# First tile of products in quarters, second pair of chunks one after the other, inverse matmuls spread over more steps

## The chip, the cores and the metric

The kernel runs on one core of a Trainium2 chip. A core has a matrix engine (TensorE, "PE"; its weight loads are listed apart as "PEld"), a vector engine (VectorE, "DVE"), an engine for activation functions (ScalarE, "ACT"), a general one (GpSimd, "POOL") and a sequencer that mostly issues transfers (SyncE, "SP"). Each works through its own instructions in order and waits at semaphores for the others. 16 DMA engines move data between DRAM and the on-chip memories SBUF and PSUM; transfers issued by SP and ACT go to hardware queues, those issued by POOL to a software queue. The metric is the device time of one execution in microseconds (us), lower is better.

## The reference

```python
xn = layernorm(x)                                  # x: 2048 x 1024, over the last axis
X  = rfft2(xn) * (w_r + 1j * w_i)                  # w_r, w_i: 2048 x 513
s  = irfft2(X, (2048, 1024))
g  = silu(silu(xn @ w1) @ w2)                      # w1: 1024 x 3584, w2: 3584 x 1024
out = x + s * g
```

All inputs and the output are float32.

## The kernel before

**Numbers.** Each float32 operand of a matmul is split into a high and a low float16 part, and three products are added: high x high, high x low, low x high. The high part is an ACT copy with a scale (`high`, line 228), the low part a DVE subtraction (`low`, line 231). Weights are scaled by powers of two per tile: `maxi` takes each row's largest magnitude on DVE, `scales` adds these maxima over the rows with a small PE matmul (line 235) and computes the scale in a few small DVE instructions (lines 256 to 265).

**Tiles.** The 2048 rows of x form four chunks c of 512 rows, each of four parts p of 128. A chunk is normalized and transposed into `xnT[c]` (high and low). Chunks 0 and 1 are transposed on PE (`trans`, then `hi` on ACT and `lo` on DVE, through two PSUM buffers "tp"); chunks 2 and 3 by DMA transposes that SP issues (`turned`, line 633). The 3584 columns of w1 form 28 tiles f of 128. A tile of the first product, `mm1(c, f)`, is 24 matmuls of 128x512 (8 slices of the inner dimension, three terms); ACT applies silu to its PSUM result (line 441) and `hidden` makes from two neighbouring f and two neighbouring chunks the sums and differences of a Strassen-like scheme, splits them ("hosum" and "hoone", one buffer each) and stores them to DRAM ("hd"). The second product, `mm2`, goes through seven such products m of eight tiles j, each in two halves of 21 matmuls; `acc` adds its results up, and `final` finishes output rows.

**Spectral part.** Forward transform along the rows (`fa_mat`, `fd_gen`), along the columns with the filter (`f_gen`), then the inverse, `i_gen(c)`, for the chunks in the order 1, 3, 0, 2. `i_gen` loads "zt" and a table, copies a few edge values into zt on ACT (line 1133), does four matmul groups `mat(0..3)` (line 1146, 48 matmuls each, PSUM tiles "iu" from the pool `pt` with two buffers), each followed by `post` (its PSUM tile is last read at line 1157), `split`, and then four groups `mat2` and `bfly` (last instruction line 1225). The edge values of all chunks come from a small job, `edge_gen`, mostly on POOL.

**Order.** The program is written out in order by one loop over `order`, the list of (c, f). After each tile (and after each half tile of `mm2`) one event takes place: ACT and DVE work left over from the last tiles is issued, then stores that are due (`tick`), then `work()` takes one step of the queue `wq` (weights), in three of four events one of `xq` (maxima, edges), and up to three of `bg` (layer norm of later chunks, forward, filter, inverse). A generator that yields PAUSE ends the event; other yields name no wait. Steps of `bg` are also held back by a count of PE and DVE time that the program keeps from its own instructions (`meter`, line 190). An instruction stands in its engine's stream where its event stands.

**The start.** Lines 1338 to 1361: x parts 0 and 1, the identity matrix, x parts 2 and 3, then raw w1 tiles 0 to 3 are loaded by SP; `spin` issues matmuls without use, 35 at first and 8, 8, 8 and 12 between the steps of layer norm and weights. Tile (0,0) is one `mm1` with all terms; in event 0 the sums of w1 tiles 2 and 3 (`scales(2, 2)`) are issued, and then tile (0,1).

**Order of tiles.** (0,0..3), (1,0..3), (0,4), (0,5), (1,4), (1,5), then for f = 0, 2, 4: (2,f), (2,f+1), (3,f), (3,f+1); then for every further pair of f all four chunks. `finish(bg, ln[c])` before a chunk's first tile forces its layer norm to be issued by then. Raw w1 tiles from 6 on are loaded only when chunk 3 has used earlier ones (`ahead`, `used1`), and w1 raw and split tiles share seven buffers.

**Stores.** `stores[0]` is the engine that issues the stores of hidden, forward and filter results; here it is POOL throughout.

Of the kernel before, what the change touches and what calls it, by code (L numbers as in the profile page):

```python
# [10 lines left out]
F32 = mybir.dt.float32  # L11
# [10 lines left out]
WARM = [35, 8, 0, 8, 0, 8, 12, 0, 0, 0]  # L22
# [82 lines left out]
def spectral_ffn(ctx, tc, x, w_r, w_i, w1, w2, ca, kc, ci, tw, pm, out):  # L105
# [40 lines left out]
    deferred, stores = [], [nc.gpsimd]  # L146
# [91 lines left out]
    def weights1():  # L238
# [30 lines left out]
        def split(i):  # L269
            new[i] = fp.tile([128, 2, 8, 128], F16, name=f"w1_{i}", tag="w1", bufs=7)  # L270
            high(new[i][:, 0], raw[i], rs[:, i:i + 1])
# [5 lines left out]
        for i in range(4):  # L277
            load(i)
        yield 0
        maxi(0)  # L280
        yield 0
        maxi(1)
        yield 0
        scales(0, 2)
        yield 0
        split(0)
        rest(0)
        yield 0
        split(1)
        rest(1)  # L290
# [133 lines left out]

    def mm1(c, f):
        ps = pf.tile([128, 512], F32, name=f"pa{c}_{f}", tag="ff")
        w, xt = w1t[f], xnT[c]
        terms = [(d, wh, xh) for wh, xh in ((0, 0), (0, 1), (1, 0)) for d in range(8)]
        if c + f:
            terms.sort(key=lambda k: k[0])  # L430
        for n, (d, wh, xh) in enumerate(terms):
            nc.tensor.matmul(ps, w[:, wh, d], xt[:, xh, d], start=(n == 0), stop=(n == 23))  # L432
        if c == 3:
            used1.add(f)
        q, g = f // 2, c // 2

        def evac():
            if (q, g) not in h32:
                h32[q, g] = H["p"].tile([128, 4, 512], F32, name=f"h32_{q}_{g}", tag="h32", bufs=2)
            hq = h32[q, g]  # L440
            nc.scalar.activation(hq[:, 2 * (c % 2) + f % 2], ps, AF.Silu, scale=s1[:, f:f + 1])  # L441
            if c % 2 and f % 2:
                return hidden(q, g)

        return evac
# [209 lines left out]
    def ln_gen(c):  # L655
# [33 lines left out]
        if c == 0:  # L689
            for p in range(2):  # L690
                stats(p)
                norm[p]()
            trans(0)
            hi(0)
            stats(2)
            norm[2]()
            trans(1)
            hi(1)
            stats(3)
            norm[3]()  # L700
            lo(0)
            yield 0
            trans(2)
            hi(2)
            lo(1)
            yield 0
            trans(3)
            hi(3)
            yield 0
            lo(2)  # L710
            lo(3)
            yield 0
            return
# [410 lines left out]
    def i_gen(c):  # L1124
        ip = C["p"]
        tt, stt = nc.vector.tensor_tensor, nc.vector.scalar_tensor_tensor
        if c != IORDER[0]:
            for _ in range(3):
                yield PAUSE
        else:  # L1130
            finish(xq, edge_job[0])
        zt, k = C["z"].pop(c), C["k"].pop(c)
        nc.scalar.activation(zt[:, :, :, :, 12, 0], zp[:, c], AF.Copy)
        yield PAUSE
# [104 lines left out]
        for i in range(6):  # L1239
            if i < 4:  # L1240
                mat(i)
            if i >= 2:
                split(i - 2)
            if 1 <= i <= 4:
                post(i - 1)
            yield 3.9 if 2 <= i <= 4 else 2
# [50 lines left out]
    with tc.manual_schedule():  # L1297
# [51 lines left out]
        for i in range(2):  # L1349
            load_x(0, i)  # L1350
        nc.sync.dma_start(ident, pm[:, 3])
        for i in range(2, 4):
            load_x(0, i)
        w1j = add(wq, weights1())
# [4 lines left out]
        for k, q in enumerate((bg, wq, bg, wq, bg, wq, wq, bg, wq)):  # L1359
            slot(q)  # L1360
            spin(WARM[1 + k])
# [10 lines left out]
        order += [(c, f + i) for f in (0, 2, 4) for c in (2, 3) for i in range(2)]  # L1372
# [4 lines left out]
        for n, (c, f) in enumerate(order):  # L1377
            left -= 1
            if f == 0 and c:
                finish(bg, ln[c])  # L1380
            if ln[3].done and n >= 22 and not f_job:
# [4 lines left out]
                add(bg, switch(B, open_i, 3, lag=2))  # L1386
# [118 lines left out]
```

## Time and profile before

| | us |
|---|---|
| median of 3 runs (lowest to highest) | 1272.59 (1272.42 to 1274.44) |
| profiled execution | 1271.76 |
| its span, first to last instruction | 1270.0 |

In the profile, busy time is given per engine. A line of a timeline has start, duration, engine, line of the program, operation, output and inputs, and in brackets the idle time of the engine before it with the instruction that ended it. Names are those of the program's tiles: "pa" is the PSUM tile of a first product, "tp" of a transpose, "iu" of an inverse group, "w1r" raw weights of w1, "jr" raw weights of w2 (both loaded from the tensor called B_w in the names), "h" a first product after silu. The table of windows gives for each stretch its length, then the busy time and count of PE, PEld, DVE, ACT and POOL, then PEclk (the TensorE clock that was granted, 1.00 is full), the DMA engines' mean busy share, and GB/s.

### The profile page before, as it was taken

How to read it: one execution, taken by the hardware profiler on the slowest of the kernel's cores; microseconds unless marked ns; L12 is line 12 of the kernel's file. 1: busy time of each engine (PE TensorE's matmuls, PEld its weight loads, DVE VectorE, ACT ScalarE, POOL GpSimd, SP SyncE). 2: the span in 40 equal slices, each digit the busy share in tenths (PEclk: the TensorE clock that was granted, in tenths of full speed). 3: DMA queues.
4: the chain of work that ended last, by engine and by line, in shares of the span. 5: the costliest groups of instructions: out<-in, count | busy, mean ns of one | idle time of the engine just before them, and what ended most of it. 6: DMA issues, size and time to landing. Idle time of an engine off the chain costs nothing. (4 is left out here: it accounts for less than half of the span.)

```text
span 1270.0 us, 20677 instructions
## 1 busy us (share of the span) xinstructions
PE 1229.6 (97%) x7759; PEld 625.0 (49%) x7759; DVE 1019.9 (80%) x2056; ACT 499.4 (39%) x672; POOL 330.1 (26%) x540
## 2 busy tenths in 40 slices
PE   8997999999999999999999999997998998999998
PEld 5543455455454444445545555544544545545544
DVE  6677889999998997565958799894776858978965
ACT  4755343434364465444534444241212212232211
POOL 1352132133454444342332021214023041010000
PEclk9998999999999999999999999999999999999999
DMA  7478366576477798776988799959388699893798
GB/s 234 129 160 212 96 199 185 159 224 190 116 272 239 227 300 297 241 226 187 223 249 261 217 274 247 263 200 331 141 252 252 225 309 318 309 358 124 265 348 292
DMA packets 155460, 296.87 MB, mean 234 GB/s; under 512 B 32048, under 2 KB 77744, under 8 KB 154848
## 3 DMA queue, kind: packets, MB, share of 16 engines
q1 hardware_dynamic: 118000, 179.82, 45.7%
q0 software_dynamic: 37216, 115.60, 28.9%
q8 instruction: 61, 1.00, 0.3%
q14 instruction: 39, 0.32, 0.1%
q10 hardware_dynamic: 144, 0.13, 0.0%
HBM read 186.97 MB, written 104.33 MB: 229 GB/s over the span
## 5 line engine op out<-in xcount | busy, mean ns | idle before, releaser
L432 PE MATMUL pa<-xnT,w 128*128 128x512 f16 x2688 | 586.5, 380 | 10.5 <-DMA xnT<-xs 6.2
L432 PEld LDWEIGHTS <-w 128*128 128x128 f16 x2688 | 262.6, 98 | 322.8 <-issue 12.5
L510 PE MATMUL pb<-w,ht 128*128 128x512 f16 (+1 forms) x798 | 299.9, 376 | 0.0
L511 PE MATMUL pb<-w,ht 128*128 128x512 f16 (+1 forms) x798 | 299.6, 375 | 0.0
L512 PE MATMUL pb<-w,ht 128*128 128x512 f16 (+1 forms) x798 | 299.5, 375 | 0.0
L512 PEld LDWEIGHTS <-ht 128*128 128x128 f16 x798 | 78.1, 98 | 91.3 <-issue 0.3
L510 PEld LDWEIGHTS <-ht 128*128 128x128 f16 x798 | 78.1, 98 | 89.6 <-issue 0.4
L511 PEld LDWEIGHTS <-ht 128*128 128x128 f16 x798 | 78.1, 98 | 87.5
L441 ACT ACTIVATE h<-pa,s 128x512 f32<-128x512 f32 x112 | 75.2, 677 | 89.3 <-PE pa L432 89.3
L231 DVE SCALAR_TENSOR_TENSOR w<-jr,sc,w 128x512 f16<-128x512 f32 x98 | 72.1, 749 | 38.7 <-ACT w L228 38.5
L228 ACT ACTIVATE w<-jr,sc 128x512 f16<-128x512 f32 x98 | 68.5, 714 | 78.9 <-DMA jr<-in_B_w_dram 72.1
L388 POOL DMA_DIRECT2D jr<-in_B_w_dram x56 | 37.5, 671 | 233.4 <-issue 175.6
L464 POOL DMA_DIRECT2D hd_sum<-hosum x56 | 41.5, 783 | 190.2 <-DVE hosum L231 75.3
L952 ACT ACTIVATE zq<-Z 128x192 f16<-128x192 f32 (+2 forms) x80 | 37.2, 543 | 104.3 <-DVE Z L218 67.2
L231 DVE SCALAR_TENSOR_TENSOR hoone<-h,hs,hoone 128x2048 f16<-128x2048 f32 x28 | 65.7, 2347 | 14.8 <-ACT hoone L228 14.8
L228 ACT ACTIVATE hosum<-hr,hs 128x1536 f16<-128x1536 f32 x28 | 44.0, 1573 | 80.3 <-DVE hr L471 62.8
L228 ACT ACTIVATE hoone<-h,hs 128x2048 f16<-128x2048 f32 x28 | 56.0, 1999 | 47.4 <-DMA hd_one<-hoone 24.9
L464 POOL DMA_DIRECT2D hd_one<-hoone x56 | 48.5, 866 | 71.8 <-DVE hoone L231 36.0
L470 DVE TENSOR_TENSOR hr<-h 128x1024 f32<-128x1024 f32 x28 | 34.2, 1223 | 39.9 <-ACT h L441 39.8
L231 DVE SCALAR_TENSOR_TENSOR hosum<-hr,hs,hosum 128x1536 f16<-128x1536 f32 x28 | 50.8, 1815 | 3.8 <-ACT hosum L228 3.8
L228 ACT ACTIVATE w<-w1r,rs 128x1024 f16<-128x1024 f32 x28 | 31.9, 1144 | 52.4 <-DVE rs L259 29.7
L591 ACT ACTIVATE pl<-pl,c 128x512 f32<-128x512 f32 (+1 forms) x26 | 17.0, 684 | 79.3 <-DVE pl L570 52.7
(215 smaller groups left out, 1815.9 us busy)
## 6 DMA issues: line engine op xcount, KB each, us to landing
jr<-in_B_w_dram POOLq DMA_DIRECT2D x84, 256.0 KB, 7.3
w1r<-in_B_w_dram SPq DMA_DIRECT2D x28, 512.0 KB, 5.9
hd_sum<-hosum POOLq DMA_DIRECT2D x56, 256.0 KB, 4.0
hd_one<-hoone POOLq DMA_DIRECT2D x56, 256.0 KB, 5.3
hd_dif<-hoone POOLq DMA_DIRECT2D x56, 256.0 KB, 5.0
w2m<-in_B_w_dram SPq DMA_DIRECT2D x28, 512.0 KB, 5.5
ht<-hd_dif SPq DMA_DIRECT2D x32, 448.0 KB, 10.3
ht<-hd_sum SPq DMA_DIRECT2D x32, 448.0 KB, 5.7
```

Source lines behind the costliest of these rows:

```text
L228: nc.scalar.activation(hi, raw, AF.Copy, scale=scale)
L231: nc.vector.scalar_tensor_tensor(lo, raw, scale, hi, op0=OP.mult, op1=OP.subtract)
L388: nc.gpsimd.dma_start(raw[n], ws[m][q] if m in ws else w2_block(m, q, 0))
L432: nc.tensor.matmul(ps, w[:, wh, d], xt[:, xh, d], start=(n == 0), stop=(n == 23))
L441: nc.scalar.activation(hq[:, 2 * (c % 2) + f % 2], ps, AF.Silu, scale=s1[:, f:f + 1])
L464: defer(1, lambda k=k, m=m: stores[0].dma_start(hd[m, g][:, :, q].rearrange("f p h s -> f p (h s)"), o[:, k].rearrange("f p h s -> f p (h ...
L470: tt(sums[:, 0:2], hq[:, 0::2], hq[:, 1::2], op=OP.subtract)
L510: nc.tensor.matmul(ps, hh[:, 0], w[:, 0], start=first, stop=False)
L511: nc.tensor.matmul(ps, hh[:, 0], w[:, 1], start=False, stop=False)
L512: nc.tensor.matmul(ps, hh[:, 1], w[:, 0], start=False, stop=last)
L591: nc.scalar.activation(o, o, AF.Silu, scale=c2)
L952: nc.scalar.activation(o[0], z, AF.Copy)
```

## The change

- The identity matrix is loaded between x parts 0 and 1, and raw w1 tile 0 ahead of x parts 2 and 3. Scales and split of w1 tiles 0 and 1 are made one tile at a time.
- Tile (0,0) is made by `quarter(p, k)`: 128 of its 512 columns (part p of the chunk) for one of the three terms k, eight matmuls of 128x128 each, into one PSUM tile. The twelve quarters are placed between the steps of layer norm and weights, and `mm1(0, 0)` issues no matmul. Idle matmuls are 35 and 8 now.
- Tiles of chunks 2 and 3 with f from 0 to 5: all four of chunk 2, then four of chunk 3, then two and two.
- `stores[0]` is SP until the layer norm of chunk 3 has been issued, then POOL.
- In `i_gen`, for all chunks but the first in order, the copy into zt is issued two pauses earlier, with three pauses behind it; steps 1 and 2 of the matmul groups end in a pause; and two more pauses come ahead of the first chunk.

```diff
--- before.py
+++ after.py
@@ -19,7 +19,7 @@
 S, D, F, DF = 2048, 1024, 3584, 513
 NFT = F // 128
 NP = NFT // 2
-WARM = [35, 8, 0, 8, 0, 8, 12, 0, 0, 0]
+WARM = [35, 8]
 LEAD, PAUSE, LAST, EARLY = 1.0, -1, 6, 2
 IORDER = (1, 3, 0, 2)
 SUMMED = (4, 5)
@@ -143,7 +143,7 @@
     turn2 = cp.tile([128, 128], F32, name="turn2")
     s_sc = small("s_sc")
 
-    deferred, stores = [], [nc.gpsimd]
+    deferred, stores = [], [nc.sync]
 
     def defer(n, fn):
         deferred.append([n, fn])
@@ -268,26 +268,26 @@
 
         def split(i):
             new[i] = fp.tile([128, 2, 8, 128], F16, name=f"w1_{i}", tag="w1", bufs=7)
+            first.setdefault("w", new[i])
             high(new[i][:, 0], raw[i], rs[:, i:i + 1])
 
         def rest(i):
             w1t[i] = w = new.pop(i)
             low(w[:, 1], raw.pop(i), rs[:, i:i + 1], w[:, 0])
 
-        for i in range(4):
+        load(0)
+        yield 0
+        for i in range(1, 4):
             load(i)
         yield 0
-        maxi(0)
-        yield 0
-        maxi(1)
-        yield 0
-        scales(0, 2)
-        yield 0
-        split(0)
-        rest(0)
-        yield 0
-        split(1)
-        rest(1)
+        for i in range(2):
+            maxi(i)
+            yield 0
+            scales(i, 1)
+            split(i)
+            yield 0
+            rest(i)
+            yield 0
         maxi(2)
         maxi(3)
         yield 0
@@ -422,14 +422,25 @@
 
     done2, ready2, chunks = [0], [-1], [0]
 
+    first = {}
+
+    def quarter(p, k):
+
+        if "ps" not in first:
+            first["ps"] = pf.tile([128, 512], F32, name="pa0_0", tag="ff")
+        sl = slice(128 * p, 128 * p + 128)
+        wh, xh = ((0, 0), (0, 1), (1, 0))[k]
+        for d in range(8):
+            nc.tensor.matmul(first["ps"][:, sl], first["w"][:, wh, d], xnT[0][:, xh, d, sl], start=(p + k + d == 0), stop=(p + k == 5 and d == 7))
+
     def mm1(c, f):
-        ps = pf.tile([128, 512], F32, name=f"pa{c}_{f}", tag="ff")
-        w, xt = w1t[f], xnT[c]
-        terms = [(d, wh, xh) for wh, xh in ((0, 0), (0, 1), (1, 0)) for d in range(8)]
+        ps = first["ps"] if c + f == 0 else pf.tile([128, 512], F32, name=f"pa{c}_{f}", tag="ff")
         if c + f:
+            w, xt = w1t[f], xnT[c]
+            terms = [(d, wh, xh) for wh, xh in ((0, 0), (0, 1), (1, 0)) for d in range(8)]
             terms.sort(key=lambda k: k[0])
-        for n, (d, wh, xh) in enumerate(terms):
-            nc.tensor.matmul(ps, w[:, wh, d], xt[:, xh, d], start=(n == 0), stop=(n == 23))
+            for n, (d, wh, xh) in enumerate(terms):
+                nc.tensor.matmul(ps, w[:, wh, d], xt[:, xh, d], start=(n == 0), stop=(n == 23))
         if c == 3:
             used1.add(f)
         q, g = f // 2, c // 2
@@ -690,24 +701,25 @@
             for p in range(2):
                 stats(p)
                 norm[p]()
-            trans(0)
-            hi(0)
+            for p in range(2):
+                trans(p)
+                hi(p)
+            yield 0
             stats(2)
+            yield 0
             norm[2]()
-            trans(1)
-            hi(1)
             stats(3)
-            norm[3]()
             lo(0)
-            yield 0
             trans(2)
             hi(2)
+            yield 0
+            norm[3]()
             lo(1)
-            yield 0
             trans(3)
             hi(3)
             yield 0
             lo(2)
+            yield 0
             lo(3)
             yield 0
             return
@@ -1124,14 +1136,14 @@
     def i_gen(c):
         ip = C["p"]
         tt, stt = nc.vector.tensor_tensor, nc.vector.scalar_tensor_tensor
-        if c != IORDER[0]:
-            for _ in range(3):
-                yield PAUSE
+        if c == IORDER[0]:
+            finish(xq, edge_job[0])
         else:
-            finish(xq, edge_job[0])
+            yield PAUSE
         zt, k = C["z"].pop(c), C["k"].pop(c)
         nc.scalar.activation(zt[:, :, :, :, 12, 0], zp[:, c], AF.Copy)
-        yield PAUSE
+        for _ in range(1 if c == IORDER[0] else 3):
+            yield PAUSE
         psu, uf, us = {}, {}, {}
 
         def mat(g):
@@ -1243,7 +1255,7 @@
                 split(i - 2)
             if 1 <= i <= 4:
                 post(i - 1)
-            yield 3.9 if 2 <= i <= 4 else 2
+            yield PAUSE if i in (1, 2) else 3.9 if i in (3, 4) else 2
         if c != IORDER[-1]:
             load_i(IORDER[IORDER.index(c) + 1])
         yield PAUSE
@@ -1346,19 +1358,44 @@
         nc.scalar.activation(warm, ones[:, 0:1], AF.Silu)
         J = {}
         open_fwd()
-        for i in range(2):
-            load_x(0, i)
+        load_x(0, 0)
         nc.sync.dma_start(ident, pm[:, 3])
+        load_x(0, 1)
+        w1j = add(wq, weights1())
+        slot(wq)
         for i in range(2, 4):
             load_x(0, i)
-        w1j = add(wq, weights1())
         slot(wq)
         ln = [add(bg, ln_gen(0)), None, None, None]
         nc.gpsimd.memset(mhalf, -0.5)
         spin(WARM[0])
-        for k, q in enumerate((bg, wq, bg, wq, bg, wq, wq, bg, wq)):
-            slot(q)
-            spin(WARM[1 + k])
+        slot(bg)
+        slot(wq)
+        slot(bg)
+        spin(WARM[1])
+        slot(wq)
+        quarter(0, 0)
+        quarter(1, 0)
+        slot(bg)
+        slot(wq)
+        quarter(0, 1)
+        slot(bg)
+        quarter(2, 0)
+        quarter(1, 1)
+        slot(wq)
+        quarter(0, 2)
+        quarter(1, 2)
+        slot(bg)
+        slot(wq)
+        quarter(3, 0)
+        quarter(2, 1)
+        quarter(2, 2)
+        slot(bg)
+        slot(wq)
+        quarter(3, 1)
+        quarter(3, 2)
+        slot(wq)
+        slot(bg)
         for i in range(4):
             load_x(1, i)
             if i == 1:
@@ -1369,7 +1406,7 @@
             add(bg, fd_gen(c))
 
         order = [(c, f) for fs in ((0, 1, 2, 3), (4, 5)) for c in range(2) for f in fs]
-        order += [(c, f + i) for f in (0, 2, 4) for c in (2, 3) for i in range(2)]
+        order += [(c, f) for fs in ((0, 1, 2, 3), (4, 5)) for c in (2, 3) for f in fs]
         order += [(c, f + i) for f in range(6, NFT - LAST, 2) for c in range(4) for i in range(2)]
         order += [(2 * g + c, f + i) for g in range(2) for f in range(NFT - LAST, NFT, 2) for c in range(2) for i in range(2)]
         last_use = {c: max(n for n, k in enumerate(order) if k[0] == c) for c in range(4)}
@@ -1378,12 +1415,14 @@
             left -= 1
             if f == 0 and c:
                 finish(bg, ln[c])
+            if ln[3].done:
+                stores[0] = nc.gpsimd
             if ln[3].done and n >= 22 and not f_job:
                 add(xq, wmax_gen())
                 max_job = add(xq, w2max_gen())
                 f_job = add(bg, switch(A, open_f, 1, max_job))
                 add(bg, f_gen())
-                add(bg, switch(B, open_i, 3, lag=2))
+                add(bg, switch(B, open_i, 5, lag=2))
                 for k in IORDER:
                     add(bg, i_gen(k))
             if left == 2 * LAST + 3:
```

## The prediction

> **What bounds the kernel now.** First the page: the span and the engines' shares.
>
> ```profile
> span 1270.0 us, 20677 instructions
> ...
> PE 1229.6 (97%) x7759; PEld 625.0 (49%) x7759; DVE 1019.9 (80%) x2056; ACT 499.4 (39%) x672; POOL 330.1 (26%) x540
> ```
>
> TensorE (PE) is busy for 97%, so the number of products bounds the kernel, and the change takes none away: 24 products of 512 columns become 96 of 128. What it can win is the 40.4 us in which PE stands (1270.0 - 1229.6) and what follows from standing. The table of PE's waits names them (us in total, times, longest):
>
> ```profile
> PE iu L1146 <- ACT zt L1133: 11.2, 3, 5.8
> PE iu L1146 <- DVE uw L1157: 6.5, 5, 3.4
> PE pa L432 <- DMA xnT<-xs: 6.2, 2, 5.7
> PE pa L432 <- ACT h L441: 1.9, 1, 1.9
> ...
> PE fa L742 <- DVE xnT L686: 1.5, 1, 1.5
> ```
>
> The first two stand ahead of and between the inverse matmuls (17.7 us), the next two around tile (3,0) of the first products (8.1 us). What follows from standing is in the windows' PEclk column, the third number from the end (the last two are the DMA share and GB/s):
>
> ```profile
> 108.00:112.00 4.00, 0.41 (x1) 0.21 (x2) 3.90 (x9) 3.48 (x3) 0.00 (x0) 0.54 1.12 236
> 114.00:117.00 3.00, 3.00 (x13) 1.23 (x12) 3.00 (x16) 0.00 (x0) 1.70 (x3) 0.81 0.21 62
> 877.00:881.00 4.00, 4.00 (x96) 3.87 (x92) 2.23 (x5) 1.32 (x2) 2.11 (x4) 0.66 1.02 394
> 962.00:970.00 8.00, 6.55 (x155) 5.10 (x156) 5.60 (x14) 1.89 (x5) 2.90 (x4) 1.00 1.07 325
> 1046.00:1050.00 4.00, 3.94 (x90) 3.94 (x92) 2.68 (x4) 0.73 (x2) 1.43 (x2) 0.62 1.09 312
> ```
>
> The stops that go with them, in PE's timeline (start, duration, in brackets the idle time before and its releaser):
>
> ```profile
> 876.83 4.22 PE L1146 MATMUL iu<-kk,zt 64*128 64x128 f16 x96 [5.79 <-ACT zt L1133]
> ...
> 962.68 2.85 PE L1146 MATMUL iu<-kk,zt 64*128 64x128 f16 x96 [2.81 <-ACT zt L1133]
> ...
> 1046.07 4.48 PE L1146 MATMUL iu<-kk,zt 64*128 64x128 f16 x96 [2.60 <-ACT zt L1133]
> ...
> 1053.95 2.74 PE L1146 MATMUL iu<-kk,zt 64*128 64x128 f16 x48 [3.41 <-DVE uw L1157]
> ```
>
> After the stops at 876 and 1046, and around (3,0), the granted clock is 0.54 to 0.81 for some microseconds; after the one at 962 it is 1.00, and the same 96 products take 2.85 there against 4.22 and 4.48. A removed stop can give back up to 1.6 beyond its own length. The 1.5 of fa stays: the statistics ahead of it keep their place behind the dense start.
>
> **The start.** Timeline, start and duration in us:
>
> ```profile
> 9.03 0.70 DVE L661 BATCH_NORM_STATS2 st<-x 128x6 f32<-128x512 f32 x1 [1.83 <-DMA x<-in_A_x_dram]
> ...
> 11.87 1.17 DVE L686 TENSOR_TENSOR xnT<-tp,xnT 128x1024 f16<-128x1024 f32 x1
> ...
> 13.02 1.00 ACT L682 ACTIVATE xnT<-tp 128x1024 f16<-128x1024 f32 x1
> ...
> 13.19 1.14 PE L678 MATMUL tp<-ident,x 128*128 128x128 f32 x8 [1.34 <-ACT x L669]
> 13.93 1.23 ACT L669 ACTIVATE x<-x,v 128x1024 f32<-128x1024 f32 x1
> ...
> 17.60 0.16 DVE L256 TENSOR_SCALAR e<-s 128x2 int32<-128x2 int32 x1 [1.18 <-PE s L235]
> ...
> 18.41 2.19 ACT L228 ACTIVATE w<-w1r,rs 128x1024 f16<-128x1024 f32 x2 [0.77 <-DVE rs L259]
> ...
> 19.59 1.28 DVE L231 SCALAR_TENSOR_TENSOR w<-w1r,rs,w 128x1024 f16<-128x1024 f32 x1 [0.83 <-ACT w L228]
> ...
> 24.25 2.34 DVE L251 TENSOR_REDUCE m<-w1r 128x1 f32<-128x1024 f32 x2
> ...
> 26.73 0.35 PE L235 MATMUL s<-m,ones 128*128 128x2 f32 x2
> ...
> 26.95 10.52 PE L432 MATMUL pa<-xnT,w 128*128 128x512 f16 x48
> ```
>
> Dense work begins at 26.95, when the column sums of w1 tiles 2 and 3 have passed PE. These sums wait for the two maxima on VectorE (DVE), at 24.25 to 26.59. After the change the sums still stand ahead of tile (0,1) on PE, and the maxima still come last on DVE, so an early first tile moves nothing unless DVE ends sooner. Its idle time before is 1.83 + 1.18 + 0.83 = 3.84; that, less some 0.9 for a second set of scales (17.60 to 18.41 and a little more), is the most that can be won: 3.0.
>
> Followed by hand, it loses. Raw w1 tile 0 now lies ahead of x2 and x3 on SP's queue. The windows in which the identity and raw w1 came in, and the first and last of 24 products of 128 columns:
>
> ```profile
> 5.00:6.00 1.00, 1.00 (x7) 0.73 (x5) 0.97 (x3) 0.00 (x0) 0.10 (x1) 1.00 0.48 82
> 11.00:12.00 1.00, 0.85 (x8) 0.51 (x6) 0.97 (x4) 0.12 (x1) 0.74 (x2) 1.00 1.16 290
> ```
>
> ```profile
> 104.37 0.22 PE L742 MATMUL fa<-cas,xnT 128*128 128x128 f16 x1
> ...
> 105.65 0.22 PE L744 MATMUL fa<-cas,xnT 128*128 128x128 f16 x1
> ```
>
> 512 KB at 290 GB/s is 1.8, so x2 lands at 10.8, not 9.0. Then, in program order: statistics 2 (1.42, half of 9.03 to 11.87) to 12.25; first scales to 13.2; statistics 3 to 14.6; lo 0 (1.17) to 15.8; trans 2 (1.14, its PSUM buffer is free only then) to 16.95; hi 2 (1.0) to 17.95; norm 3, now behind hi 2 on ACT (1.23), to 19.2; trans 3 to 20.35; four quarters, which PE runs in order ahead of the next sums, to 22.15 (8 products of 0.056, 1.28 for 23, are 0.45 a quarter); sums (0.35) and second scales (17.60 to 19.59 - 0.83, 1.16) to 23.75 with the handoffs; lo 3 to 24.9; rest 1 (1.28) to 26.2; two maxima (2.34) to 28.5; sums, and dense work at 28.9: **1.9 later**. Further, the identity matrix now lies ahead of x1. The second that carries it in the trace (5 to 6 us) moved 82 GB/s; if x1 inherits this gap of some 1.7 us, its transpose holds PE and with it the first scales: 3.6 later. The 28 idle matmuls taken out (20 + 8) were behind a wait in any case. But with them gone PE has holes of up to 2.6 us here, and a low clock costs 0 to 1.6 (4.48 - 2.85). The range is -3.0 to +5.2; I take **+3.0**, nearest to the rows that carry the two queue moves.
>
> [...]
>
> **Chunk 2 ahead of chunk 3.** PE, and the ACT instruction that held the chain:
>
> ```profile
> 99.19 5.34 PE L432 MATMUL pa<-xnT,w 128*128 128x512 f16 x24 [1.89 <-ACT h L441]
> ...
> 111.59 0.58 PE L432 MATMUL pa<-xnT,w 128*128 128x512 f16 x1 [5.72 <-DMA xnT<-xs]
> 112.66 5.69 PE L432 MATMUL pa<-xnT,w 128*128 128x512 f16 x20 [0.48 <-DMA xnT<-xs]
> ```
>
> ```profile
> 96.56 2.00 ACT L228 ACTIVATE hoone<-h,hs 128x2048 f16<-128x2048 f32 x1 [8.09 <-DMA hd_one<-hoone]
> ```
>
> ```profile
> 151.39 20.88 PE L432 MATMUL pa<-xnT,w 128*128 128x512 f16 x96
> ```
>
> A tile is 24 x 0.2175 = 5.2. Tile (3,0) moves two tiles back: PE asks for the transposed chunk 3 at 97.3 (99.19 - 1.89) + 5.2 + 1.3 (fa) + 10.4 = 114.2, and it was there at 112.66. So 6.2 goes. ACT's 8.09 is a wait for hidden stores that POOL issued; it delayed the evacuation that cost PE 1.89, and chunk 3's normalization as well. These stores move to SP until chunk 3 is through, past POOL's statistics, so both come earlier: 1.9 goes. The clock's surplus at 112.66 is 5.69 - 20 x 0.2175 = 1.3, of which 0.15 is a modelled end. **-9.3** in all. SP pays: its stores wait for DVE, and the transposes of chunk 3 stand behind them. The sum has 1.5 us of room for that (114.2 - 112.66), and what ACT gains. The fewer idle matmuls also set back the planner's count of PE time, so background steps can come an event later here; chunk 2's have the cover of tiles 4 to 11.
>
> The other side of the order: loads of w1 tiles 6 and up are released by chunk 3's uses, now two tiles later.
>
> ```profile
> L231 DVE SCALAR_TENSOR_TENSOR w<-w1r,rs,w x2: 1277/1279/1281, 156.3 to 165.2; 128x1024 f16<-128x1024 f32 x2
> ```
>
> These are the lows of tiles 6 and 7; tile (0,6) starts three tiles after 151.39, at 167. Tile 6 has 9.4 of room, tile 7 (needed at 172.2) 5.7. Their steps move by one to two tiles of 5.2, and two hidden splits that were four tiles apart on ACT are now two apart, as were those around the 8.09. A stop of 0 to 8 (the 8.09); I take **+1.5**, since POOL is free of statistics there.
>
> **Inverse matmuls.** The ACT instruction ahead of the first copy:
>
> ```profile
> 872.59 0.72 ACT L228 ACTIVATE w<-jr,sc 128x512 f16<-128x512 f32 x1 [10.33 <-DMA jr<-in_B_w_dram]
> ```
>
> The small copy zt stands on ACT behind weight splits that wait for their loads. For three chunks it is issued two events earlier and the matmuls stay; an event is half a product tile, 21 x 0.2175 = 4.6, so 9.1 of lead against waits of 2.8. For the first chunk everything moves two events back: 9.1 against 5.79, but its copy carries the same ACT queue along, so part may stay. The third and fourth matmul groups each get an event of 4.6 ahead of them, against waits of at most 3.41 for uw. The surplus of the low clock is 4.22 - 2.85, 4.48 - 2.85 and 2.74 less half of 2.85: 4.3. All gone would be 11.2 + 6.5 + 4.3 = 22.0; I leave 4.0 standing, most of it at the first chunk (bounds 0 and 15): **-18.0**.
>
> **The end.** Last inverse result, and the window after the last product:
>
> ```profile
> L1225 DVE SCALAR_TENSOR_TENSOR s<-so,spq x16: 419/421/422, 920.7 to 1208.4; 128x256 f32<-128x256 f32 x16
> ```
>
> ```profile
> 1264.00:1270.00 6.00, 0.00 (x0) 0.00 (x0) 2.95 (x8) 0.91 (x2) 0.00 (x0) 0.90 0.33 115
> ```
>
> Two more pauses at the start and up to one more in each of four chunks push the inverse back by 2 to 6 events, 9 to 27 us, to 1218 to 1236 on the old clock; products run until 1264, so it is hidden. Its stores then fall among the last products' loads: 0 to 4, I take **+1**.
>
> **Sum:** 3.0 - 9.3 + 1.5 - 18.0 + 1 = -21.8, a span of 1248.2. The profiled execution took 1271.76, 1.76 over its span, and is 0.8 under the median of 1272.59: **1250**.
>
> **Rivals.** (a) The start gains 3.0 instead of losing: 1244. For it: the first scales no longer wait for tile 1. Against: DVE's order above. (b) Transposes held up on SP: all but the 1.9 stays, 1257.5. [...] (c) ACT's queue moves along: half of the inverse waits stay (9 more than the 4.0) and tile 6 stops PE for 6: 1263. For it: 10.33 for one load, 8.09 for one store. (d) Slower: chunk 2 of the inverse slips past the last product, where each event costs its 4.6 openly. It has (1264 - 1208)/4.6 = 12 events of room, and with 21.8 gained elsewhere decides only from some 17 events on; at 18, 1276 to 1280. Against it: 2 to 6 events counted. (e) The spacing and the order do nothing on balance: 1271.
>
> **How the numbers follow.** Forecast 0.54 (1245 to 1256), (a) 0.11, (b) 0.09, (c) 0.16 (0.02 of it within 0.2%), (e) 0.03, (d) 0.07. 0.2%, 2.5 us, is about what a measurement of this kernel can tell from no change. Faster 0.54 + 0.11 + 0.09 + 0.14 = 0.88, same 0.05, slower 0.07. The range leaves out (d), (e) and the ends of (a) and (c): 1241 to 1265.
>
> **What would show it.** Right: first 48-product run of L432 at 29 to 30; no PE wait for xnT<-xs; zt and uw waits together under 5; PEclk 1.00 through 860 to 1150. Wrong: dense work before 27, a PE wait for w L231 or ACT w near 165, PE waits for zt of the old size, or DVE work of the inverse after 1250.

## The result, and the profile after

| | before | after |
|---|---|---|
| median, us (runs) | 1273.18 (4, beside the changed kernel) | 1253.16 (4) |
| lowest to highest | 1272.42 to 1274.44 | 1251.81 to 1256.74 |
| profiled execution, its span | 1271.76, 1270.0 | 1256.74, 1254.9 |

The ratio is 0.9846 (95% interval 0.9823 to 0.9869): 20.0 us faster. The profiled execution is the slowest of the four, 3.6 over the median. Four landmarks on TensorE (PE) split its span: the first matmul of the forward transform (fa), the first second product (pb), the last matmul, and the end.

| us | fa | fa to pb | pb to PE's end | behind it | span |
|---|---|---|---|---|---|
| before | 47.7 | 603.1 | 613.1 | 6.1 | 1270.0 |
| after | 54.1 | 593.9 | 599.1 | 7.8 | 1254.9 |
| difference | +6.4 | -9.2 | -14.0 | +1.7 | -15.1 |

So the start lost, the two stretches behind it won, and the end lost a little. First the page after, span and engines:

```profile
span 1254.9 us, 20766 instructions
...
PE 1227.9 (98%) x7805; PEld 625.1 (50%) x7805; DVE 1020.4 (81%) x2061; ACT 499.6 (40%) x672; POOL 322.1 (26%) x526
```

PE stands for 27.0 us (1254.9 - 1227.9) in place of 40.4. Its waits in the kernel after (us in total, times, longest):

```profile
PE tp L689 <- ACT x L680: 4.9, 3, 1.7
PE iu L1158 <- DVE uw L1169: 3.7, 2, 2.4
PE s L235 <- DVE m L251: 2.5, 1, 2.5
PE fx L924 <- DMA vq<-vd: 2.1, 1, 2.1
PE pa L434 <- ACT w L228: 2.0, 1, 2.0
PE fa L754 <- DVE xnT L697: 1.5, 1, 1.5
...
PE pa L443 <- DVE w L231: 0.7, 1, 0.7
```

The waits for zt, for xnT by transposes and for h are gone, and those for uw fell from 6.5 to 3.7. New are one of the column sums for the maxima "m" (2.5), one of the first quarters for the high part of w1 tile 0 (2.0) and 0.7 for w1 tile 6; the start's transposes now wait 4.9 for normalized x instead of 2.6, and the filter matmul "fx" 2.1 instead of 0.3. The timeline of the kernel after shows the first of these, and the windows what it does to the clock:

```profile
9.47 1.22 DVE L251 TENSOR_REDUCE m<-w1r 128x1 f32<-128x1024 f32 x1 [0.72 <-DMA w1r<-in_B_w_dram]
...
13.55 0.16 DVE L256 TENSOR_SCALAR e<-s 128x1 int32<-128x1 int32 x1 [1.26 <-PE s L235]
...
24.46 0.16 DVE L256 TENSOR_SCALAR e<-s 128x1 int32<-128x1 int32 x1 [3.00 <-PE s L235]
...
27.82 2.34 DVE L251 TENSOR_REDUCE m<-w1r 128x1 f32<-128x1024 f32 x2
...
30.30 0.56 PE L235 MATMUL s<-m,ones 128*128 128x2 f32 x2 [2.49 <-DVE m L251]
...
30.72 13.16 PE L443 MATMUL pa<-xnT,w 128*128 128x512 f16 x48
...
54.10 0.22 PE L754 MATMUL fa<-cas,xnT 128*128 128x128 f16 x1 [1.47 <-DVE xnT L697]
```

```profile
19.00:29.00 10.00, 6.09 (x91) 5.61 (x89) 6.86 (x15) 4.32 (x4) 0.00 (x0) 1.00 0.35 133
29.00:30.00 1.00, 0.00 (x0) 0.00 (x0) 1.00 (x2) 0.00 (x0) 0.00 (x0) 0.63 0.43 113
30.00:36.00 6.00, 5.70 (x15) 2.37 (x16) 4.18 (x14) 1.15 (x1) 0.17 (x1) 0.50 0.28 83
36.00:37.00 1.00, 1.00 (x5) 0.39 (x4) 0.90 (x3) 0.00 (x0) 0.81 (x3) 0.95 1.10 326
60.00:130.00 70.00, 70.00 (x363) 33.41 (x362) 56.25 (x115) 46.12 (x41) 20.63 (x25) 1.00 0.76 182
...
877.00:881.00 4.00, 4.00 (x30) 1.79 (x30) 0.00 (x0) 0.00 (x0) 2.50 (x4) 1.00 1.07 307
```

Tile (0,0) begins early, but dense work, 48 products in a row, begins at 30.72, 3.77 later than before, and they take 13.16 in place of 10.52, since PE runs at 0.50 for 6 us: 3.77 + 2.64 = the 6.4 at fa. This is not the first low clock of the new start: PE also ran at 0.50 from 15.6 to 19.0. VectorE (DVE) runs the maxima of w1 tiles 2 and 3 (27.82) behind the second, separate set of scales, and for that set it waits 3.00, as its column sum stands on PE behind a transpose and four quarters. From 60 to 130, where PE used to stand for chunk 3, and at 877, where it stood for zt, it now works without a gap at full clock. Two stretches of 0.50 are left later on: from 776.8 to 780.2, behind the filter's stop, and from 1063.5 to 1066.9, behind a wait of 2.42 for uw.

### The profile page after: what moved, and what is told of

Read it like the earlier page. It is cut to its first block, busy times and chain, and to the rows that moved or that the text cites. A ratio compares the mean times of both kernels' runs of the same rounds, so it can differ in the third digit from the quotient of the medians.

```text
span 1254.9 us, 20766 instructions
## 1 busy us (share of the span) xinstructions
PE 1227.9 (98%) x7805; PEld 625.1 (50%) x7805; DVE 1020.4 (81%) x2061; ACT 499.6 (40%) x672; POOL 322.1 (26%) x526
## 5 line engine op out<-in xcount | busy, mean ns | idle before, releaser
L231 DVE SCALAR_TENSOR_TENSOR w<-jr,sc,w 128x512 f16<-128x512 f32 x98 | 71.9, 745 | 33.6 <-ACT w L228 33.5
L475 POOL DMA_DIRECT2D hd_sum<-hosum x52 | 38.2, 772 | 180.5 <-DVE hosum L231 116.7
L231 DVE SCALAR_TENSOR_TENSOR hoone<-h,hs,hoone 128x2048 f16<-128x2048 f32 x28 | 65.6, 2343 | 11.2 <-ACT hoone L228 11.2
L231 DVE SCALAR_TENSOR_TENSOR hosum<-hr,hs,hosum 128x1536 f16<-128x1536 f32 x28 | 50.7, 1811 | 3.4 <-ACT hosum L228 3.4
L228 ACT ACTIVATE w<-w1r,rs 128x1024 f16<-128x1024 f32 x28 | 31.9, 1143 | 47.7 <-DVE w L231 26.4
```

What stands on the lines that cost most here:

```text
L228: nc.scalar.activation(hi, raw, AF.Copy, scale=scale)
L231: nc.vector.scalar_tensor_tensor(lo, raw, scale, hi, op0=OP.mult, op1=OP.subtract)
L475: defer(1, lambda k=k, m=m: stores[0].dma_start(hd[m, g][:, :, q].rearrange("f p h s -> f p (h s)"), o[:, k].rearrange("f p h s -> f p (h ...
```

## The experiments

Each kernel was timed beside the kernel before on its chip, whose medians lie between 1273.05 and 1274.08.

| kernel | median, us (lowest to highest) | ratio to before (95% interval) |
|---|---|---|
| e1_old_start | 1246.07 (1245.13 to 1246.51) | 0.9780 (0.9766 to 0.9795) |
| e2_inverse_only | 1257.03 (1255.98 to 1258.75) | 0.9869 (0.9853 to 0.9884) |
| e3_order_only | 1268.06 (1265.44 to 1269.91) | 0.9952 (0.9937 to 0.9968) |
| e4_stores_only | 1268.00 (1266.74 to 1271.22) | 0.9956 (0.9941 to 0.9970) |
| e8_no_spacing | 1263.21 (1262.27 to 1268.18) | 0.9928 (0.9912 to 0.9944) |
| e5_spins_in_hole | 1255.56 (1251.55 to 1257.38) | 0.9855 (0.9837 to 0.9873) |
| e6_ident_after_x1 | 1253.78 (1252.07 to 1257.36) | 0.9852 (0.9834 to 0.9870) |
| e7_sums_inside | 1257.61 (1254.27 to 1258.65) | 0.9874 (0.9857 to 0.9890) |
| e9_sums_inside2 | 1252.87 (1250.77 to 1254.45) | 0.9837 (0.9817 to 0.9856) |
| e10_ident_spins | 1252.28 (1250.01 to 1252.97) | 0.9829 (0.9810 to 0.9848) |
| e11_after_again | 1256.34 (1255.99 to 1258.86) | 0.9868 (0.9849 to 0.9887) |
| e12_old_start_wider | 1241.58 (1239.65 to 1243.50) | 0.9742 (0.9717 to 0.9767) |

### The parts one by one: e1 to e4 and e8

**e1_old_start** is the kernel before with every part of the change but the start: the three diffs of e2, e3 and e4 together. Its edit against the changed kernel, in parts:

```diff
-WARM = [35, 8]
+WARM = [35, 8, 0, 8, 0, 8, 12, 0, 0, 0]
...
-        slot(wq)
-        quarter(0, 0)
-        quarter(1, 0)
...
+        for k, q in enumerate((bg, wq, bg, wq, bg, wq, wq, bg, wq)):
+            slot(q)
+            spin(WARM[1 + k])
```

> The changed kernel with the start of before: one whole tile (0,0), scales of w1 tiles 0 and 1 together, all idle matmuls, loads in the old order. The order of tiles, the stores and the inverse stay changed. Theory A (the start of the change loses: dense products began at 30.72 instead of 26.95, and their first 48 took 13.16 instead of 10.52 at a granted clock of 0.50, together 6.4): about 1247, 6 under the changed kernel's 1253.2, with dense products from 27 on, 48 of them in 10.5, and the first product of the forward transform (fa) back near 47.7. Theory B (the delay is made up for further on, since background steps are given out by a count of PE and DVE time, not by the chip's): within 2 of 1253.

It is 7.1 us faster than the changed kernel, and its four runs lie within 1.4 us: theory A. Its timeline:

```profile
26.30 10.52 PE L432 MATMUL pa<-xnT,w 128*128 128x512 f16 x48
...
47.04 0.22 PE L742 MATMUL fa<-cas,xnT 128*128 128x128 f16 x1 [1.47 <-DVE xnT L686]
```

The difference at fa, 54.10 - 47.04 = 7.1, is as large as that of the medians, and nothing of it is regained behind. That the two agree so closely is in part chance: the medians come from two chips (by the ratios to before the difference is 8.4), and the two profiled executions differ by 10.3, 7.1 of it at fa and 3.2 behind it.

**e2_inverse_only**: the kernel before with the edits of the inverse alone.

```diff
-            for _ in range(3):
-                yield PAUSE
...
+            yield PAUSE
...
-        yield PAUSE
+        for _ in range(1 if c == IORDER[0] else 3):
+            yield PAUSE
...
-            yield 3.9 if 2 <= i <= 4 else 2
+            yield PAUSE if i in (1, 2) else 3.9 if i in (3, 4) else 2
...
-                add(bg, switch(B, open_i, 3, lag=2))
+                add(bg, switch(B, open_i, 5, lag=2))
```

> Before with the edits of the inverse alone: the copy into zt earlier, steps 1 and 2 of the matmul groups ending in a pause, two more pauses ahead of the first chunk. Theory A (the waits and the low clock behind them make nearly all of the gain): PE waits for zt gone, 3 to 5 of the 6.5 for uw gone, clock 1.00 after each: 1255 to 1257, 16 to 18 under before. Theory B (ACT's queue moves along with the steps and half of the waits come back): 1262 to 1266. The 6.2 for xnT and the 1.9 for h stay in both.

PE's waits in e2_inverse_only:

```profile
PE pa L432 <- DMA xnT<-xs: 6.7, 2, 6.0
PE iu L1146 <- DVE uw L1157: 3.2, 2, 2.4
...
PE pa L432 <- ACT h L441: 2.0, 1, 2.0
```

The zt waits are gone, 3.2 for uw is left, and chunk 3 still stops PE: 16.6 us from this part by itself, theory A.

**e8_no_spacing**: the same without the pauses at steps 1 and 2.

```diff
-            yield PAUSE if i in (1, 2) else 3.9 if i in (3, 4) else 2
+            yield 3.9 if 2 <= i <= 4 else 2
```

> Before with the edits of the inverse but without the pauses at steps 1 and 2: copies into zt earlier, first chunk two pauses later. All edits of the inverse together gave 1257.0, before is 1273.7. Theory A (the two kinds of wait are separate; the lead of the copies takes the 11.2 for zt and 3.0 of low clock, the pauses the rest): waits for zt gone, for uw 5 to 7, 1259 to 1261. Theory B (uw's waits come from matmul groups that start late behind zt; with zt on time they go by themselves): uw under 4, 1256 to 1258. Theory C (the pauses carry the gain, since the copy moves with the ACT queue anyway): zt waits of 4 or more, 1264 or more.

```profile
1056.90 2.74 PE L1146 MATMUL iu<-kk,zt 64*128 64x128 f16 x48 [5.91 <-DVE uw L1157]
```

This line of PE's timeline in e8_no_spacing is the largest of five waits for uw, 9.1 us together. The earlier copies take the zt waits away (9.8 us), but the next wait in line grows behind them; the two pauses are worth 6.8 more (16.6 - 9.8). The time lies between theories A and C; uw at 9.1 is more than A or B expected.

**e3_order_only** and **e4_stores_only**:

```diff
-        order += [(c, f + i) for f in (0, 2, 4) for c in (2, 3) for i in range(2)]
+        order += [(c, f) for fs in ((0, 1, 2, 3), (4, 5)) for c in (2, 3) for f in fs]
```

```diff
-    deferred, stores = [], [nc.gpsimd]
+    deferred, stores = [], [nc.sync]
...
+            if ln[3].done:
+                stores[0] = nc.gpsimd
```

> Before with the new order of tiles alone (chunk 2's four tiles, then chunk 3's); the stores stay on POOL. Theory A (the two tiles of cover are enough, as the transposes landed at 112.66 and PE would ask at 114): the 6.2 wait for xnT goes and the low clock behind it, the 1.9 for h stays; 1265 to 1267. Theory B (the stores on SP are needed too, since ACT's wait for hidden stores holds chunk 3's normalization): 2 to 5 of the 6.2 stay, 1269 to 1272. A wait of PE for w1 tile 6 near 165, if the order alone makes it, shows here as well.

> Before with the early stores on SP alone; the order of tiles stays. Theory A (SP issues them earlier than POOL did, but the transposes of chunk 3 now stand behind them): the 1.9 for h goes, the wait for xnT stays between 3 and 8; 1269 to 1273. Theory B (the earlier stores free ACT by so much that the transposes come in time): both go, 1264 to 1266. Theory C (in one ring with the transposes the stores hold them up): the wait for xnT grows over 8, 1275 or more.

PE's timeline in e3_order_only:

```profile
99.37 7.03 PE L432 MATMUL pa<-xnT,w 128*128 128x512 f16 x24 [2.71 <-ACT h L441]
```

PE's timeline in e4_stores_only:

```profile
107.12 0.58 PE L432 MATMUL pa<-xnT,w 128*128 128x512 f16 x1 [3.58 <-ACT hoone L228]
...
108.37 8.90 PE L432 MATMUL pa<-xnT,w 128*128 128x512 f16 x30 [0.66 <-DMA xnT<-xs]
```

Each part removes one of the two stops and leaves the other, as theory A of each has it (the times came 1.1 above and 1.0 below its ranges): the order alone keeps the late evacuation, and the tile behind it takes 7.03 in place of 5.34; the stores alone let PE's second product of chunk 3 start at 108.37 in place of 112.66, and PE still waits 3.58 + 0.66 around its first product. What the stores do to the transposes shows in SP's queue in e4_stores_only (start, time to issue):

```profile
90.79 6.50 SPq L633 DMA_TRANSPOSE xnT<-xs  x4
97.39 0.54 SPq L464 DMA_DIRECT2D hd_one<-hoone  x1
97.99 1.34 SPq L464 DMA_DIRECT2D hd_dif<-hoone  x2
99.37 0.66 SPq L464 DMA_DIRECT2D hd_one<-hoone  x1
100.56 5.82 SPq L633 DMA_TRANSPOSE xnT<-xs  x4
```

The same queue in the kernel before:

```profile
80.23 30.48 SPq L633 DMA_TRANSPOSE xnT<-xs  x8
```

ScalarE's timeline in e4_stores_only:

```profile
91.10 2.00 ACT L228 ACTIVATE hoone<-h,hs 128x2048 f16<-128x2048 f32 x1 [5.19 <-DMA hd_one<-hoone]
```

The stores do hold transposes up. ScalarE has written the high part of chunk 3's third part by 96.84, and its transposes are issued from 100.56 on, behind four stores (97.39 to 100.03); in the kernel before it was written by 102.31 and its transposes began at 102.34. But ScalarE's wait for a store, 8.09 before, is 5.19 and ends 5.5 earlier (91.10 against 96.56), which is more: the last transposes are issued by 106.4, without the stores by 110.7. These rows show SP's order of issue; in what order the transfers then ran no row shows. Single gains add up: 16.6 + 5.6 + 5.7 = 27.9 against 27.6 for e1, all against the same runs of before. In the profiled executions the stretch from fa to pb, where both parts act, is 5.0 shorter in e3, 3.0 in e4 and 10.6 in e1 against e2, so the agreement of the sums is partly chance.

### The start: e5, e6, e7, e9, e10, e11

**e5_spins_in_hole** is the changed kernel with the stop at 27.8 to 30.3 filled, **e6_ident_after_x1** with the identity behind x1:

```diff
         quarter(3, 2)
+        spin(22)
         slot(wq)
```

```diff
         load_x(0, 0)
-        nc.sync.dma_start(ident, pm[:, 3])
         load_x(0, 1)
+        nc.sync.dma_start(ident, pm[:, 3])
```

> The changed kernel with 22 idle matmuls (0.109 each, 2.4 in all) behind the last quarter, where PE stood 2.49 ahead of the column sums of w1 tiles 2 and 3. Theory A (that stop is what brings the granted clock to 0.50 from 29.6 to 36, which costs 2.64): the first 48 dense products take 10.5 instead of 13.16, dense work still begins at 30 to 31, fa moves from 54.1 to 51.5: 1250 to 1251. Theory B (the sparse work of all the start brings the clock down, so that 2.4 of work at its end changes nothing): 48 products stay at 13, 1253. Theory C (idle matmuls hold the sums up): dense work at 32 or later, 1254 or more.

> The changed kernel with the identity matrix loaded behind x1 again, still ahead of raw w1 tile 0. Theory A (the identity's slow transfer made DVE wait 1.19 for x1, and PE's transpose of x1 held the first scales by as much): x1's statistics follow x0's at once, dense work begins 1.0 to 1.5 earlier, at 29.2 to 29.7, 1252. Theory B (the gap only passes to raw w1 tile 0 and x2, which come as late as before and hold DVE instead): dense work at 30.4 to 31, 1253.

PE's timeline in e5_spins_in_hole:

```profile
30.29 10.52 PE L443 MATMUL pa<-xnT,w 128*128 128x512 f16 x48
...
456.24 3.07 PE L443 MATMUL pa<-xnT,w 128*128 128x512 f16 x9 [2.17 <-ACT h L452]
```

PE's timeline in e6_ident_after_x1:

```profile
28.27 13.06 PE L443 MATMUL pa<-xnT,w 128*128 128x512 f16 x48
```

The cause of this low clock is shown: with idle matmuls in the hole the granted clock is 1.00 from 30 to 36 and the same 48 products take 10.52, as theory A of e5 has it. That the identity delays the start is shown as well, but not by how much: dense work begins 2.45 earlier in e6 than in the changed kernel, 1.19 earlier in e10 than in e5 (29.10 against 30.29) and 3.07 earlier in e10 than in e11 (32.17), and two profiles of the changed kernel itself differ by 1.45. Between e6 and the changed kernel the 2.45 can be split. The first quarters begin at 13.99 and 15.52, 1.5 apart; the other 0.9 is made by PE at a clock of 0.50 from 15.6 to 19.0 in the changed kernel, where these 16 products and the transpose behind them take 1.84 and 1.92 instead of 1.07 and 1.13. In time neither expectation came: neither median can be told from that of the changed kernel. In e5's profiled execution a stop at 456 takes back part of what was won, and it is in no other run.

**e7_sums_inside** and **e9_sums_inside2** give the maxima cover instead: the sums, scales and split of w1 tiles 2 and 3 are issued behind the 12th product of tile (0,1); e9 moves the background steps of event 0 behind them as well.

```diff
+                if (c, f, n) == (0, 1, 12):
+                    slot(wq)
                 nc.tensor.matmul(ps, w[:, wh, d], xt[:, xh, d], start=(n == 0), stop=(n == 23))
...
-                slot(wq)
+                if n:
+                    slot(wq)
```

```diff
                     slot(wq)
+                    slot(queues['bg'])
+                    slot(queues['bg'])
...
-                for _ in range((2, 0, 1, 1)[f]):
+                for _ in range((0, 0, 1, 1)[f]):
```

> The changed kernel with the sums, scales and split of w1 tiles 2 and 3 issued in the middle of tile (0,1), after 12 of its 24 products, instead of ahead of it. Theory A (PE stands at 27.8 only because the sums lie ahead of work that is ready): tile (0,1) starts at 28, the stop of 2.49 and the low clock behind it go, tile (0,2) waits under 1 for the lows of w1 tile 2, fa at 49 to 50: 1248 to 1249.5, most of the 7.1 that the start costs. Theory B (w1 tile 2 then comes as much later as tile (0,1) comes earlier, and PE stands ahead of (0,2) instead): a wait of 2 or more for w L231 there, 1252 to 1253.

DVE and PE in the timeline of e7_sums_inside:

```profile
35.97 0.10 DVE L256 TENSOR_SCALAR e<-s 128x2 int32<-128x2 int32 x1
...
37.92 1.03 PE L447 MATMUL pa<-xnT,w 128*128 128x512 f16 x2 [4.72 <-ACT w L228]
```

Theory A missed, and a wait of theory B's kind came, by the experiment's own placement: statistics of chunk 1, issued ahead of the scales, hold DVE until these begin at 35.97, and tile (0,2) waits 4.72 for its weights. That asked for e9:

> The changed kernel with the sums, scales and split of w1 tiles 2 and 3 issued behind the 12th product of tile (0,1), as in e7_sums_inside, and the two background steps of event 0 (statistics of chunk 1) moved to the same place, behind the scales. Theory A (what the early first tile loses is the 2.49 us stop for the maxima of tiles 2 and 3 and the low clock behind it): dense products from 27.8 without a stop, no wait over 1.5 ahead of (0,2), granted clock 1.00 from 30 on, fa at 49 to 50.5 against 54.10, and the time 1247 to 1250. Theory B (the early first tile loses more than that, later on, because statistics of chunks 1 to 3 and the splits are set back against PE): fa at 49 to 50.5 but new stops behind fa, 1251 to 1255.

Windows of e9_sums_inside2 (PE alone, then PEclk, DMA share, GB/s):

```profile
27.00:30.00 3.00, 2.02 (x23) 1.00 0.00 0
30.00:33.00 3.00, 3.00 (x16) 1.00 0.60 175
```

The stop and the low clock are gone, and fa falls to 51.40, 3.1 earlier than the changed kernel on the same chip (54.48, e11), which is given below; in both of these profiles the last quarters lay 1.3 to 1.6 later than in the first one, behind two stretches of 0.50 between 11 and 22 us. The time falls by as much, 3.5, which is theory A in kind; in absolute terms it is B's 1251 to 1255, without new stops between fa and pb (593.3 us).

**e10_ident_spins** is e5 and e6 together, **e11_after_again** the changed kernel unaltered.

```diff
         load_x(0, 0)
-        nc.sync.dma_start(ident, pm[:, 3])
         load_x(0, 1)
+        nc.sync.dma_start(ident, pm[:, 3])
...
+        spin(22)
         slot(wq)
```

> The changed kernel with both edits of e5_spins_in_hole and e6_ident_after_x1: x part 1 ahead of the identity matrix, and 22 idle matmuls ahead of the sums of w1 tiles 2 and 3. Theory A (the two losses of the start add up): the first 48 products take 10.5 instead of 13.16 and begin at 28.3 to 28.7, fa at 48.8 to 49.3, and the time is 1247 to 1250, one to four above the old start (1246.07). Theory B (what is gained ahead of fa is lost behind it, as in the profiled run of e5_spins_in_hole): fa as in A, but stops of 3 to 6 in sum between fa and the second products, 1252 to 1256.

> The changed kernel once more, on the chip of the two runs beside it. Both theories: 1252 to 1255, with 3 to 5 us between its runs. Theory A of the spread (it belongs to the new start, whose low clock and stops differ between runs): the profiled run has fa at 53 to 55 again and stops behind it that are not those of the run before. Theory B (the spread belongs to the chip): under 2 us between runs here.

PE's timeline in e11_after_again:

```profile
32.17 12.09 PE L443 MATMUL pa<-xnT,w 128*128 128x512 f16 x48
```

In e10_ident_spins fa stands at 49.84, 4.6 earlier than in e11, and the time is 4.1 better; this is theory A in kind and B in the time. It still is 0.9829 of before against 0.9780 for e1, 6.2 us. The profiled spans differ by 5.95 (1250.6 against 1244.65). At fa e10 is 2.8 behind e1; most of the rest comes at one stop, which PE's timeline in e10_ident_spins shows:

```profile
772.57 0.37 PE L924 MATMUL fx<-vq,kq 128*128 128x256 f16 x1 [3.83 <-DVE yb L1021]
```

The window around it in e10_ident_spins:

```profile
770.00:775.00 5.00, 2.43 (x18) 2.09 (x19) 4.93 (x10) 1.03 (x2) 0.54 (x1) 0.69 1.03 401
```

The same window in e1_old_start:

```profile
770.00:775.00 5.00, 5.00 (x35) 2.71 (x33) 4.97 (x11) 1.64 (x4) 0.54 (x1) 1.00 1.05 399
```

The filter matmul waits 3.83 in e10 and 2.27 in e1, 1.56 more, and with the clock at 0.69 behind it the stretch from pb to PE's end is 2.95 longer (600.05 against 597.1). DVE is full in both windows (4.93 and 4.97 of 5), but the profile names another releaser in each kernel (yb on DVE in e10, xc on ACT in e1, a load of vq in the changed kernel), so what ends last there is not settled. Behind the start the two programs issue the same kinds of instructions in the same order on every engine, and e12 below, whose program is that of e1 up to this point, waited only 0.51. So this stop varies with the moment at which PE arrives; it is 1.6 to 3.8 in the seven profiles with the new start and at most 2.3 in those with the old one. What sets its length stays open, and so does how much of the 6.2 it makes in the runs without a profile. e11 came out 1.3 above its expected upper end, with 2.9 between its runs, under the 3 to 5 expected; its profiled fa, 54.48, is close to the 54.10 of the first profile, though dense work began 1.45 later and its 48 products lost 1.07 less to the clock. The cause of the spread between runs was not found.

No variant of the new start reaches e1: e10 and e9, the best of them, stay 6 to 7 above it.

### One step further: e12

**e12_old_start_wider** is e1 with a wider spacing where uw still stopped PE:

```diff
+            if c == 0 and i in (1, 2):
+                yield PAUSE
             yield PAUSE if i in (1, 2) else 3.9 if i in (3, 4) else 2
```

> e1_old_start with one pause more ahead of the third and of the fourth group of inverse matmuls of chunk 0, where two waits for uw (0.94 and 2.42 us) and a granted clock of 0.83 behind them are left. Theory A (each pause puts another half product tile of 4.6 us between the preparation and its matmuls, and what waits for uw is only DVE's and ACT's lead): both waits go, PE does not stop between 780 and the last product, and the time falls by 3.4 and up to 1.2 for the clock, 1241 to 1243. Theory B (uw is late because DVE's work between the groups moves along with the pause): both waits stay in size, 1245 to 1247. Theory C (the pauses push the chunk's later groups and chunk 2 into the end): DVE's last inverse result after 1225, 1247 or more.

A window of e1_old_start:

```profile
1050.00:1060.00 10.00, 7.58 (x70) 4.29 (x69) 8.77 (x19) 2.26 (x3) 0.00 (x0) 0.83 0.99 365
```

The window of e12_old_start_wider over the third and fourth group:

```profile
1044.00:1060.00 16.00, 16.00 (x117) 7.80 (x116) 14.59 (x34) 2.65 (x4) 0.00 (x0) 1.00 0.99 365
```

Theory A: the waits and the low clock are gone, and at 0.9742 it is the fastest of all, 32 us under the kernel before and some 4.5 under e1. Some of the latter is not the pauses' doing: in the profiles the filter's stop near 770, which they do not touch, is 0.51 in e12 and 2.27 in e1.

## Why the prediction was right, and where it was not

The forecast case came: 1253.16 lies in its 1245 to 1256, 3.2 over the 1250 taken (with both additions that it names, 1.76 and 0.8, its sum is 1250.8). That it came so near is partly luck: the start was priced 4.1 too low and the order with the stores 3.2 too low in gain, and the two nearly cancel. The terms, one by one:

| term | predicted | measured | from |
|---|---|---|---|
| start | +3.0 (-3.0 to +5.2) | +7.1 | e1 against after |
| order and stores, with tile 6 | -9.3 + 1.5 = -7.8 | -11.0 | e1 against e2 |
| inverse | -18.0 | -16.6 | e2 |
| end | +1 | +1.7 | PE's end to the span's end |

The first three rows add to -20.5 against the measured -20.0; the end, read from the profile, is contained in what e2 measured and is not added again.

**The start is the mis-sized term**, outside its own bounds (at fa the two profiles with the same other parts differ by 7.1). Its mechanism was followed rightly: sums for tiles 2 and 3 stay ahead of tile (0,1), and PE stands for the maxima. The hand-followed chain holds where the identity is out of the way: 28.9 by hand, 28.27 in e6. The 3.6 with the identity's gap meets the 3.77 of the first profile, but by luck in part, since dense work of the same kernel began 5.2 later in e11; taking 3.0 threw some of it away. What failed is the price of the clock, "0 to 1.6", taken from stops in the inverse. The low clock came twice in the new start. From 15.6 to 19.0 it costs 0.9 of the 3.77, by the split given for e6; the prediction has no such loss among the steps it follows, and sets the idle matmuls taken out at nothing, as they were behind a wait in any case. With the old start, and so with them, one of seven profiles has such a stretch between 10 and 22 us, with the new start six of seven; that the idle matmuls are the reason is not tested. From 29.3 to 36.1 it costs 2.64 (13.16 - 10.52), as e5 shows by filling the hole. With the 1.3 by which dense work begins later in e6 than in the kernel before, and the identity's 1.5, this makes the 6.4 at fa: 1.3 + 1.5 + 0.9 + 2.6. Nor does the length of a stop alone give the clock's price: 2.49 came with a clock of 0.50 here, the 2.81 at 962 in the kernel before with 1.00. The gap of the identity was put at 1.7; the first quarters of e6 and the changed kernel are 1.5 apart. Without the identity ahead of x1 and without the later low clock (e10) 2.8 is left at fa against e1, where 1.9 was predicted for raw w1 tile 0 ahead of x2 and all that follows.

**Order and stores** came out 3.2 better. The two stops of 6.2 and 1.9 went and their clock with them, as said; each part alone brings about half of it (e3, e4). Part of the surplus is tile 6, priced at 1.5: it costs 0.7 in the kernel after, nothing in e1. The rest is that the stops are longer in e2, from which this row is measured: 6.7 and 2.0, and the stretch from fa to pb is 10.6 shorter in e1.

**The inverse** came as forecast in size, with the rest elsewhere: 4.0 was left standing "most of it at the first chunk". That chunk has no stop any more; the 3.7 left is for uw in chunk 0, the third. The half product tile per pause holds: e8 without the pauses, e12 with more of them. Of the signs that the prediction names for being right two failed: the clock is not 1.00 throughout 860 to 1150, but 0.50 for 3.4 us behind the 2.42 for uw, and dense work at 29 to 30 came at 30.72. Of those for being wrong one showed, a wait for w L231 at 164.6, 0.7 long.

**The rivals.** (a) and (e) are excluded by e1 and e2. (b) did not come: in e4 the stores hold transposes up, but ScalarE gains more than that, and in the kernel after no wait for them is left. (c) did not occur: no zt wait is left and tile 6 has 0.7. (d) has no part in it: the last inverse result on DVE in the kernel after stands at 1210.3, 37 us ahead of the last product.

```profile
L1237 DVE SCALAR_TENSOR_TENSOR s<-so,spq x16: 414/415/420, 921.5 to 1210.3; 128x256 f32<-128x256 f32 x16
```

Not foreseen was the filter's stop near 775, 0.35 in the kernel before and 2.1 in the kernel after, which goes up to 3.8 (e10).

## What to carry to other kernels

Work moved ahead of a wait won nothing here, as the wait stayed: look for what ends last behind it (here the maxima on DVE) and move that first, or give it cover. Count a hole on PE at its length plus the clock it may cost (2.64 with the stop of 2.49 in the kernel after). Where the hole could not go, filling it kept the clock at 1.00 behind it (e5 and e10; 2.64 in the profile of e5), though no gain in time could be told from that alone. When terms are added up, check whether a close result comes from errors that cancel. Where a wait is for a small preparation on another engine, issue it a known number of product tiles earlier, then look for the next wait in line; it can grow when the first one goes (uw from 6.5 to 9.1 in e8).

## What the runs showed of the hardware

In the kernel after, a stop of 2.49 us behind sparse work (PE busy for 1.54 of the 5 us up to 30.30) came with a granted clock of 0.50 from 29.3 to 36.1, and the 48 products behind it took 13.16. They took 13.06 in e6, behind the same stop of 2.49, and 12.09 in e11, against 10.52 in the kernel before, so the surplus was 2.64, 2.54 and 1.57. The length of the last stop alone does not tell the clock behind it:

| kernel, stop (us, its end) | granted clock behind it |
|---|---|
| before, 2.81 to 962.68 | 1.00 (962 to 970) |
| before, 2.60 to 1046.07 | 0.62 (1046 to 1050) |
| after, 2.49 to 30.30 | 0.50 (30 to 36) |
| e9, 3.01 to 773.31 | 1.00 (its fx products of 128x256 from 758 to 792 all took 0.27) |
| after, 2.10 to 775.76 | 0.50 (776.8 to 780.2) |

What decides between the two is not settled here.

With 22 idle matmuls of about 0.12 us each in the hole the clock behind it was 1.00 (e5 from 30 to 36, e10 from 30 to 50). With the identity matrix, a transfer of 64 KB, ahead of x1 on the queue, dense work began 1.2 to 3.1 us later in three pairs of profiles.
